# Packed attention, mixture of experts and soft mixture of experts in one fp32 kernel: the fold matrix made early, 4 KB weight rows and 32-row output matmuls in the tail

## The chip, the cores and the metric

One core of one Trainium2 chip runs the whole program. The metric is the device time of one execution in microseconds (us), the median of several runs. The kernel before the change was timed at 516.65 us (three runs, 515.19 to 517.91). TensorE (PE) multiplies, with PEld as its weight loads; VectorE (DVE), ScalarE (ACT) and GpSimd (POOL) do the rest, and SyncE (SP) issues nearly all DMAs.

## What is computed

```python
def sm_attn(qq, kk, vv):                      # softmax(q k^T / 8) v
    s = scale * np.matmul(qq, kk.transpose(0, 1, 3, 2))
    a = np.exp(s - np.max(s, axis=-1, keepdims=True))
    a = a / (np.sum(a, axis=-1, keepdims=True) + 1e-09)
    return np.matmul(a, vv)
p_packed = sm_attn(p, k, v)                   # 4 batches, 8 heads, 576 tokens, 32 packed, 64 wide
x = sm_attn(q, p_packed, p_packed)            # -> (2304, 512)

p = domain_probs / (domain_probs.sum(-1, keepdims=True) + 1e-09)
for e in range(4):                            # moe_w1 (4, 512, 1024), moe_w2 (4, 1024, 512)
    out += p[:, e:e+1] * (np.maximum(x @ w1[e], 0) @ w2[e])
x = out

logits = x @ phi                              # 32 slots = 8 experts x 4
d = softmax(logits, over the 2304 tokens);  slot_input = d.T @ x
slot_out[e] = np.maximum(slot_input[e] @ m1[e], 0) @ m2[e]     # m1 (8, 512, 1024), m2 (8, 1024, 512)
c = softmax(logits, over the 32 slots);     result = c @ slot_out          # (2304, 512)
```

All inputs and the output are fp32. In the program `w1`, `w2` are the weights of the first expert layer, `m1`, `m2` those of the second.

## The kernel before

The hidden values of the first expert layer are made in 128 slots: 4 batches (`b`), 8 chunks of 512 hidden columns each, 4 slots of 128 columns to a chunk. PE computes a slot in `mm1` (L620), ACT, DVE and POOL apply the ReLU and the gate (`ht`, L625 to L631), DVE turns the result (`flip_h`, L641) into `hr`, a ring of five places (`place(b, i)`), and PE adds to the logits (`logits`, L653). `softmaxes` (L677 and on) and `pooling` (L775) of a batch run inside the next batch's slots; `pooling` adds `d^T h` into `tacc`. `w2` isn't applied to tokens: it is multiplied with phi at the start (for the logits) and with the pooled `tacc` at the end.

For the last batch softmax and pooling have no later slots to hide in. That is the tail, in program order:

- `pooling(3)` on PE, then four DVE operations (L789) that rescale `tacc` and add;
- the rest of the last softmax: DVE (L743), POOL (L745), ACT (L749), DVE (L751 to L753), POOL (L755), DVE (L758) into `cts`;
- POOL makes `fold` (L1114), two stacked identities that add the two halves of the 128 partitions, then `sel` and zeros;
- **tt**: 16 matmuls of `tacc` with `fold` (L1133), in two halves of 8, copied out by DVE and by ACT (L1139);
- **si**: `tt` times `w2` (L1146), 32 matmuls; then `st2` (L1160 to L1175);
- **hid**: `st2` times `m1` (L1201), ReLU, eight transposes (`hidt`, L1219), `hm`;
- **so**: `hm` times `m2` (L1246): for experts 0 to 3 at the full width of 512 columns, for experts 4 to 7 in two parts of 256 columns. After each part come `so_sb`, `sr` (a matmul with `sel` that repeats the slots in four groups of 32 rows), `rr`, and the outputs: 18 matmuls with `ct` (L1284), copies to SBUF (`drain`, ACT and DVE in turn) and six DMAs of 384 KB.

The outputs use fp32r, a shortened format: in the trace an fp32r matmul leaves one record, an fp32 matmul two (the 16 of tt are 32 records). To keep fp32's precision, `ct` and `rr` are split in a high and a low part: the four 32-row groups hold hi, hi, lo, lo of `ct` against hi, lo, hi, lo of `rr`, so one 128-row matmul adds four products.

The tail's weights (`w2`, `m1`, `m2`) come as one stream of 80 chunks of 512 KB, on SP's queue in a fixed order: chunks 0 to 15 are `w2`, 16 to 47 `m1`, 48 to 63 the first half of `m2`, 64 to 71 and 72 to 79 the two parts of its second half. They use places of SBUF that come free (39 slots in all, `add_slots`). `fill_stream` starts them during the last batch; once all slots are taken, `load_chunk` issues chunk 39 and on, four at a time, when four chunks have been multiplied. So the first reload waits for the first eight matmuls of si, and SP, which works in order, holds everything behind it. A chunk of `w2` is read as two rows of 2 KB per partition, of `m1` as one of 4 KB, of `m2` as two of 2 KB (first half) or four of 1 KB:

```python
w2[e, 128 * x : 128 * x + 256, :].rearrange("(x p) d -> p x d", p=128)
```

`leftover(p, n, k)` is the end of ring place `p`, which no chunk uses.

Of the kernel before, what the change touches and what calls it, by code (L numbers as in the profile page):

```python
# [18 lines left out]
def tile_packed_attention_moe_softmoe(  # L19
# [102 lines left out]
    def place(b, i):  # L122
        return (NE * b + i) % RING
# [681 lines left out]
    for x in range(0, NFT, 2):  # L805
        for e in range(NE):
            chunks.append(
                w2[e, 128 * x : 128 * x + 256, :].rearrange("(x p) d -> p x d", p=128)
            )
# [72 lines left out]
    with tc.manual_schedule():  # L882
# [157 lines left out]
        for s in range(nslot):  # L1040
# [21 lines left out]
            if last == 0:  # L1062
                att.close()
                open_stream("s1", "right")
                for _ in range(2):
                    add_slots(1, a2_place)
            elif last == 8:
                hr_slots([place(NB, 0)])
            elif last == SPB - 3:
                add_slots(2, w1_place)  # L1070
# [27 lines left out]
        for _ in sg[b]:  # L1098
# [5 lines left out]
        tt = fin.tile([128, 2, NFT, 64], F32, tag="tt", name="tt")  # L1104
        ct = fin.tile([128, NB // 2, XR, 2, 2, 32], F32R, name="ct")
        rr_t = fin.tile([128, DM], F32R, name="rr")
        st2 = [
# [4 lines left out]
        sel = fin.tile([128, 128], F32, name="sel")  # L1112
        fold = fin.tile([128, 2, 32], F32, name="fold")
        pool.tensor_tensor(  # L1114
            out=fold,
            in0=ident.rearrange("p (a b s) -> p a b s", a=2, b=2)[:, :, 0],
            in1=ident.rearrange("p (a b s) -> p a b s", a=2, b=2)[:, :, 1],
            op=ALU.add,
        )
        si = leftover(0, DM)  # L1120
# [60 lines left out]

        chi = fin.tile([128, DF], F32R, tag="tt", name="chi")[:, :S]
        act.copy(chi, cts)
        for b in range(NB):
            src, hi = (
                t[32 * b : 32 * b + 32].rearrange("p (r x t) -> p x r t", r=2, t=32)
                for t in (cts, chi.bitcast(F32))
            )
# [26 lines left out]
        for i in range(2):  # L1215
            ps = mm_ps(f"hidt{i}")
            for j in range(4):
                o = 512 * i + 128 * j
# [21 lines left out]
        for s, d0, dw in so_steps:  # L1240
# [24 lines left out]
            act.copy(rr, sr[:, :dw])  # L1265
            for r0 in (32, 96):
                dve.tensor_tensor(  # L1267
                    out=rr[r0 : r0 + 32], in0=sr[r0 : r0 + 32, :dw],
                    in1=rr[r0 : r0 + 32].bitcast(F32), op=ALU.subtract,
                )  # L1270
            nb, nt = 512 // dw, 3
            for b2 in range(NB // 2):
# [4 lines left out]
                for j0 in range(0, XR, nt):  # L1277
                    jn = min(XR - j0, nt)
                    ob = out_tile()
                    for j in range(j0, j0 + jn, nb):  # L1280
                        m = min(nb, j0 + jn - j)
                        ps = mm_ps(f"o{d0}_{b2}_{j}")
                        for jl in range(m):
                            pe.matmul(  # L1284
                                ps[:, dw * jl : dw * jl + dw], cv[:, j + jl], rr,
                                start=True, stop=True,
                            )
                        drain(ob[:, dw * (j - j0) : dw * (j - j0 + m)], ps[:, : dw * m])
                    sp.dma_start(
# [33 lines left out]
```

## Time and profile before

| | us |
|---|---|
| median of three runs | 516.65 |
| the profiled execution, its own time | 512.97 |
| its span, first to last instruction | 511.2 |
| PE busy | 467.6 (91%) |
| DVE / POOL / ACT busy | 295.0 / 204.4 / 185.4 |
| mean granted TensorE clock | 0.962 of full speed |

The profiled execution is 3.68 us under the median of the runs. Nearly all idle time of PE lies in the tail, from about 419 us on; before it PE works without a gap (the stretch from 290 to 415 us shows 124.97 of 125 us busy). The tail has to be read on two lines at once: what PE waits for, and whether the 16 DMA engines move data. Times in rows are from the span's start.

### The profile page before, as it was taken

How to read it: one execution, taken by the hardware profiler on the slowest of the kernel's cores; microseconds unless marked ns; L12 is line 12 of the kernel's file. 1: busy time of each engine (PE TensorE's matmuls, PEld its weight loads, DVE VectorE, ACT ScalarE, POOL GpSimd, SP SyncE). 2: the span in 40 equal slices, each digit the busy share in tenths (PEclk: the TensorE clock that was granted, in tenths of full speed). 3: DMA queues.
4: the chain of work that ended last, by engine and by line, in shares of the span. 5: the costliest groups of instructions: out<-in, count | busy, mean ns of one | idle time of the engine just before them, and what ended most of it. 6: DMA issues, size and time to landing. Idle time of an engine off the chain costs nothing.

```text
span 511.2 us, 13177 instructions
## 1 busy us (share of the span) xinstructions
PE 467.6 (91%) x5572; PEld 332.1 (65%) x5572; DVE 295.0 (58%) x551; ACT 185.4 (36%) x446; POOL 204.4 (40%) x266
## 2 busy tenths in 40 slices
PE   6899899999999989999998999999999985999683
PEld 3778767778775767787665877865878755322142
DVE  4674346688762977778278788754866533140022
ACT  2476445434432433455133445432443200320023
POOL 3024333458743635595244449642765505000000
PEclk8799999999999999999998999999999996899986
DMA  8999634555430555732234522591934499699997
GB/s 200 388 315 288 255 131 140 139 133 166 139 112 3 164 159 147 184 132 86 82 130 130 131 83 83 179 345 58 357 136 165 163 346 418 267 403 394 385 382 251
DMA packets 61836, 104.36 MB, mean 204 GB/s; under 512 B 5904, under 2 KB 24848, under 8 KB 61776
## 3 DMA queue, kind: packets, MB, share of 16 engines
q1 hardware_dynamic: 61648, 103.36, 59.9%
q8 instruction: 44, 0.72, 0.6%
q0 software_dynamic: 128, 0.15, 0.2%
q14 instruction: 16, 0.13, 0.1%
HBM read 98.78 MB, written 4.72 MB: 202 GB/s over the span
## 4 chain that ended last, share of the span: by engine, by line
PE 69%; DMA 17%; DVE 6%; SPq 3%; ACT 2%; issue 1%; POOL 1%; ACTq 0%; POOLq 0%; DVEq 0%
PE h L620 36%; DMA w<-in_moe_w_dram 8%; PE pb L775 8%; PE lg L653 6%; PE g L585 6%; DMA hr<-in_moe_w_dram 4%; DMA ck<-in_moe_w_dram 3%; SPq L849 2%; PE w2t L260 2%; PE sa L358 2%; PE so L1246 1%; DMA hr<-in_v_dram 1%; PE tt L1133 1%; PE o L1284 1%; PE pw L275 1%; PE pv L455 1%
## 5 line engine op out<-in xcount | busy, mean ns | idle before, releaser
L631 POOL TENSOR_TENSOR ht<-ht,pe 128x288 f32<-128x288 f32 x192 | 153.0, 806 | 180.3 <-ACT ht L630 180.2
L620 PEld LDWEIGHTS h<-a,g 128*128 128x128 f32 x1536 | 206.6, 188 | 23.0 <-issue 14.6
L620 PE MATMUL h<-a,g 128*128 128x288 f32 x1536 | 221.6, 299 | 0.0
L630 ACT ACTIVATE ht<-h 128x288 f32<-128x288 f32 x192 | 79.0, 412 | 173.8 <-PE h L620 166.2
L641 DVE STREAM_TRANSPOSE hr<-ht 128x576 f32<-128x576 f32 x128 | 97.3, 763 | 45.2 <-POOL ht L631 41.8
L597 DVE TENSOR_TENSOR g<-g,g 128x512 fp32r<-128x512 f32 x64 | 40.9, 679 | 26.0 <-ACT g L595 26.0
L625 DVE SCALAR_TENSOR_TENSOR ht<-h,pe 128x288 f32<-128x288 f32 x64 | 28.0, 438 | 37.8 <-PE h L620 37.8
L595 ACT CAST g<-g 128x512 fp32r<-128x512 f32 x64 | 34.5, 589 | 28.5 <-PE g L585 28.5
L775 PE MATMUL pb<-hr,d 32*32 32x512 f32 x1152 | 40.6, 598 | 0.0
L585 PE MATMUL g<-w,pkn 64*32 64x512 f32 x512 | 35.8, 600 | 4.2 <-DMA w<-in_moe_w_dram 4.1
L653 PE MATMUL lg<-ht,wphi 128*32 128x288 f32 x512 | 38.3, 412 | 0.0
L653 PEld LDWEIGHTS lg<-ht,wphi 128*32 128x32 f32 x512 | 13.5, 109 | 33.2 <-POOL ht L631 22.5
L775 PEld LDWEIGHTS pb<-hr,d 32*32 32x32 f32 x1152 | 18.9, 103 | 14.3 <-issue 9.2
L1246 PE MATMUL so<-hr,hm 128*32 128x256 f32 (+1 forms) x136 | 18.5, 458 | 4.6 <-DMA hr<-in_moe_w_dram 4.6
L1267 DVE TENSOR_TENSOR rr<-sr,rr 32x256 fp32r<-32x256 f32 x4 | 1.7, 424 | 34.5 <-ACT rr L1265 34.5
L267 ACT COPY hr<-w2t 128x512 f32<-128x512 f32 x32 | 17.5, 598 | 5.3 <-PE w2t L260 5.2
L260 PE MATMUL w2t<-ident,hr 128*128 128x128 f32 x128 | 18.1, 288 | 0.2 <-ACT hr L267 0.2
L260 PEld LDWEIGHTS w2t<-ident,hr 128*128 128x128 f32 x128 | 15.4, 149 | 2.9 <-issue 0.9
L673 POOL COPY ps<-dpn 128x576 f32<-128x576 f32 x16 | 10.7, 667 | 13.5 <-DVE dpn L195 13.5
L789 DVE SCALAR_TENSOR_TENSOR tacc<-tacc,rsc,pb 128x512 f32<-128x512 f32 x12 | 8.2, 744 | 13.2 <-PE pb L775 13.2
L1246 PEld LDWEIGHTS so<-hr,hm 128*32 128x32 f32 x136 | 6.1, 116 | 13.5 <-DMA hr<-in_moe_w_dram 9.3
L1133 PE MATMUL tt<-fold,tacc 128*128 128x64 f32 x32 | 7.1, 423 | 7.7 <-POOL fold L1114 7.7
(161 smaller groups left out, 444.8 us busy)
## 6 DMA issues: line engine op xcount, KB each, us to landing
w<-in_moe_w_dram SPq DMA_DIRECT2D x32, 1024.0 KB, 5.1
hr<-in_moe_w_dram SPq DMA_DIRECT2D x40, 512.0 KB, 8.8
ck<-in_moe_w_dram SPq DMA_DIRECT2D x38, 512.0 KB, 7.6
hr<-in_moe_w_dram SPq DMA_DIRECT2D x8, 1024.0 KB, 9.9
k<-in_k_dram SPq DMA_DIRECT2D x16, 288.0 KB, 4.4
v<-in_v_dram SPq DMA_DIRECT2D x18, 192.0 KB, 6.3
q<-in_q_dram SPq DMA_DIRECT2D x12, 288.0 KB, 2.9
out_dram<-ob SPq DMA_DIRECT2D x8, 384.0 KB, 5.6
```

The lines of the kernel that those rows point to most:

```text
L260: pe.transpose(st[x][:, 128 * dc : 128 * dc + 128], t[:, x, 128 * dc : 128 * dc + 128], ident,)
L585: pe.matmul(ps[g][c : c + 32, :], pkn_t[b][o : o + 64, g, hp, 0, :], t[o : o + 64, 2 * g + hp, :], start=True, stop=True, tile_position=(o ...
L595: act.copy(gg[:, 0, g], ps[g])
L597: dve.tensor_tensor(out=gg[:, 1, g], in0=ps[g], in1=gg[:, 0, g].bitcast(F32), op=ALU.subtract)
L620: pe.matmul(ps[:, :HS], gg[:, l, g, fs], m[:, ts], start=(g == 0 and i == 0), stop=(g == 1 and i == 2),)
L625: dve.scalar_tensor_tensor(out=ht[:, ts], in0=ps[:, :HS], scalar=0.0, in1=pr[:, ts], op0=ALU.max, op1=ALU.mult,)
L630: act.activation(out=ht[:, ts], in_=ps[:, :HS], func=AF.Relu)
L631: pool.tensor_tensor(out=ht[:, ts], in0=ht[:, ts], in1=pr[:, ts], op=ALU.mult)
L641: dve.transpose(out=hr[:, place(b, i), :, f0 : f0 + 32], in_=ht_t[s].rearrange("p (x t) -> p x t", t=32),)
L653: pe.matmul(lg_t[b][r][32 * x : 32 * x + 32, :HS], wphi[:, NFT * e + 4 * hf + x, :], ht_t[4 * ci + x][:, HS * r : HS * r + HS], start=(ch ...
L775: pe.matmul(pb[c][m : m + 32, :], d[o, x + par, :], hr[o, lo : hi + 1 : hi - lo, x + par, :], start=(x == 0), stop=(x == NBLK - 2), tile_p ...
L1246: pe.matmul(so[32 * e : 32 * e + 32, d0 : d0 + dw], hm[s][:, x + xl, e, :], cks[e][:, dw * xl : dw * xl + dw], start=(s == 0 and x + xl == 0),
```

## The change

Four edits:

1. `fold` is made by POOL in slot 8 of the last batch, in the leftover of ring place 1, and no longer in the `fin` pool after the softmax.
2. `w2` chunks and those of the first half of `m2` are read as one row of 4 KB per partition (neighbouring rows of the matrix). So that the rows of `tt` and `hm` match, tt's stationary operand takes every second column of two blocks of `tacc`, and hidt's takes every fourth column of `hid`. The parts of `m2`'s second half keep 1 KB rows, of four neighbouring matrix rows.
3. The outputs are plain fp32: a matmul has 32 rows, three of them (tokens j, j+1, j+2 of a group) stand in row groups 0, 32 and 64 of the array and write three PSUM banks. The hi/lo split, `chi` and the two DVE subtractions on `rr` go; `ct` holds for each row group only its own third.
4. Each output matmul has its own copy of 256 columns, ACT and DVE in turn: nine each instead of six of 512 (ACT) and six of 256 (DVE) for one part.

```diff
-                w2[e, 128 * x : 128 * x + 256, :].rearrange("(x p) d -> p x d", p=128)
+                w2[e, 128 * x : 128 * x + 256, :].rearrange("(p x) d -> p x d", x=2)
...
-                    m2[4 * s + e, 128 * x : 128 * (x + nx), d0 : d0 + dw].rearrange(
-                        "(x p) d -> p x d", p=128
-                    )
+                    m2[4 * s + e, 512 * (x // 4) : 512 * (x // 4) + 512, d0 : d0 + dw].rearrange(
+                        "(p x) d -> p x d", x=4
+                    )[:, x % 4 : x % 4 + nx]
...
                 hr_slots([place(NB, 0)])
+                fold = leftover(place(NB, 0), 64)
+                pool.tensor_tensor(
+                    out=fold.rearrange("p (a s) -> p a s", a=2),
...
+                    op=ALU.add,
+                )
...
-        fold = fin.tile([128, 2, 32], F32, name="fold")
-        pool.tensor_tensor(
-            out=fold,
...
-                    tacc[:, NFT * e2 + x].rearrange("p a b -> p (a b)"),
-                    fold.rearrange("p a s -> p (a s)"),
+                    tacc[:, NFT * e2 + x // 2 * 2 : NFT * e2 + x // 2 * 2 + 2].rearrange(
+                        "p a b c -> p (a b c)"
+                    )[:, x % 2 : 256 : 2],
+                    fold,
...
-        chi = fin.tile([128, DF], F32R, tag="tt", name="chi")[:, :S]
-        act.copy(chi, cts)
+        nt = 3
         for b in range(NB):
...
-            for c in range(4):
+            src = cts[32 * b : 32 * b + 32].rearrange("p (r x t) -> p x r t", r=2, t=32)
+            for c in range(nt):
                 dst = ct[32 * c : 32 * c + 32, b // 2, :, b % 2]
-                if c < 2:
-                    act.copy(dst, src)
-                else:
-                    dve.tensor_tensor(out=dst, in0=src, in1=hi, op=ALU.subtract)
+                (act.copy if b % 2 else dve.tensor_copy)(dst[:, c::nt], src[:, c::nt])
...
-                pe.transpose(ps[:, 128 * j : 128 * j + 128], hid[:, o : o + 128], ident)
+                pe.transpose(
+                    ps[:, 128 * j : 128 * j + 128], hid[:, 512 * i + j : 512 * i + 512 : 4], ident
+                )
...
             act.copy(rr, sr[:, :dw])
-            for r0 in (32, 96):
-                dve.tensor_tensor(
-                    out=rr[r0 : r0 + 32], in0=sr[r0 : r0 + 32, :dw],
-                    in1=rr[r0 : r0 + 32].bitcast(F32), op=ALU.subtract,
-                )
...
-                    for j in range(j0, j0 + jn, nb):
-                        m = min(nb, j0 + jn - j)
-                        ps = mm_ps(f"o{d0}_{b2}_{j}")
-                        for jl in range(m):
-                            pe.matmul(
-                                ps[:, dw * jl : dw * jl + dw], cv[:, j + jl], rr,
-                                start=True, stop=True,
-                            )
-                        drain(ob[:, dw * (j - j0) : dw * (j - j0 + m)], ps[:, : dw * m])
+                    ps = [mm_ps(f"o{d0}_{b2}_{j0}_{j}", keep=True) for j in range(jn)]
+                    for j in range(jn):
+                        o = slice(32 * j, 32 * j + 32)
+                        pe.matmul(
+                            ps[j][:, :dw], cv[o, j0 + j], rr[o], start=True, stop=True,
+                            tile_position=(32 * j, 0),
+                        )
+                    for j in range(jn):
+                        drain(ob[:, dw * j : dw * j + dw], ps[j][:, :dw])
+                    let_go(ps)
```

How the change moves instructions is shown at two places. The first is POOL. At the tail of the kernel before, `fold` stands between the last softmax product (L755, `lt`) and `sel`:

```order
L631 TENSOR_TENSOR ht_5450<-ht_5450,pe_5173 128x288
L745 TENSOR_TENSOR lt_5527<-lt_5527,cm_5701 128x576
L755 TENSOR_TENSOR lt_5527<-lt_5527,cm_5701 128x576
L1114 TENSOR_TENSOR fold<-ident 128x64
L1124 COPY sel<-ident 128x16 x8
L1170 MEMSET hr 128x256 x4
L1172 MEMSET hm_5718 128x1024
```

In the changed kernel `sel` follows the softmax product at once:

```order
L631 TENSOR_TENSOR ht_5451<-ht_5451,pe_5174 128x288
L745 TENSOR_TENSOR lt_5528<-lt_5528,cm_5702 128x576
L755 TENSOR_TENSOR lt_5528<-lt_5528,cm_5702 128x576
L1124 COPY sel<-ident 128x16 x8
L1172 MEMSET hr 128x256 x4
L1174 MEMSET hm_5719 128x1024
```

and `fold` (written into `hr`) stands in slot 8 of the last batch, between the gate products (L631) of two slots:

```order
L631 TENSOR_TENSOR ht_4697<-ht_4697,pe_4323 128x288 x2
L631 TENSOR_TENSOR ht_4767<-ht_4767,pe_4323 128x288
L631 TENSOR_TENSOR ht_4840<-ht_4840,pe_4569 128x288 x2
L1070 TENSOR_TENSOR hr<-ident 128x64
L631 TENSOR_TENSOR ht_4892<-ht_4892,pe_4569 128x288
L745 TENSOR_TENSOR lt_4545<-lt_4545,cm_4886 128x576
```

So `fold` has moved ahead of the last 29 rows of POOL's list that belong to the slots and to the last softmax. The sixteen matmuls of tt stand at the same place on PE as before.

The second place is PE in the last part's outputs. Before, the 18 matmuls are in pairs that share a bank, and singles (o, first number the pair of batches, second the first token group):

```order
L1284 MATMUL o_0_5_6143<-rr,ct 128x256
L1284 MATMUL o_0_6_6147<-rr,ct 128x256 x2
L1284 MATMUL o_0_8_6151<-rr,ct 128x256
L1284 MATMUL o_1_0_6155<-rr,ct 128x256 x2
L1284 MATMUL o_1_2_6159<-rr,ct 128x256
L1284 MATMUL o_1_3_6163<-rr,ct 128x256 x2
L1284 MATMUL o_1_5_6167<-rr,ct 128x256
L1284 MATMUL o_1_6_6171<-rr,ct 128x256 x2
L1284 MATMUL o_1_8_6175<-rr,ct 128x256
```

Now each has its own bank (o, last number the row group):

```order
L1273 MATMUL o_0_3_0_6142<-rr,ct 128x256
L1273 MATMUL o_0_3_1_6143<-rr,ct 128x256
L1273 MATMUL o_0_3_2_6144<-rr,ct 128x256
L1273 MATMUL o_0_6_0_6152<-rr,ct 128x256
L1273 MATMUL o_0_6_1_6153<-rr,ct 128x256
L1273 MATMUL o_0_6_2_6154<-rr,ct 128x256
L1273 MATMUL o_1_0_0_6162<-rr,ct 128x256
L1273 MATMUL o_1_0_1_6163<-rr,ct 128x256
L1273 MATMUL o_1_0_2_6164<-rr,ct 128x256
```

The number of matmuls and of output DMAs has not changed; the copies behind them have (nine on ACT and nine on DVE for a part).

## Rows read from the trace of the kernel before

**Rows 1.** The chain of waits from 410 us: start us, us, what

```profile
410.14 8.75 PE pb L775 x250
419.00 2.72 DVE tacc L789 x4
...
426.11 1.15 POOL lt L755
```

**Rows 2.** Stretches of the tail: from:to us, busy us (x) by engine, PEclk, DMA share, GB/s

```profile
420.00:424.00 4.00, 0.00 (x0) 0.00 (x0) 2.68 (x6) 0.02 (x1) 1.16 (x1) 1.00 1.02 409
428.00:434.00 6.00, 6.00 (x30) 6.00 (x30) 1.08 (x4) 0.00 (x0) 3.41 (x11) 0.50 1.03 419
434.00:441.00 7.00, 7.00 (x49) 2.77 (x52) 0.00 (x0) 0.59 (x1) 0.00 (x0) 0.72 0.39 142
435.00:436.00 1.00, 1.00 (x5) 0.29 (x7) 0.00 (x0) 0.30 (x1) 0.00 (x0) 0.50 0.34 139
439.00:440.00 1.00, 1.00 (x13) 0.33 (x8) 0.00 (x0) 0.00 (x0) 0.00 (x0) 1.00 0.55 127
441.00:450.00 9.00, 7.77 (x75) 3.00 (x71) 4.90 (x14) 5.94 (x9) 0.00 (x0) 1.00 1.03 414
451.00:471.00 20.00, 18.98 (x141) 5.28 (x134) 2.65 (x6) 0.93 (x3) 0.00 (x0) 1.00 1.05 397
471.00:492.00 21.00, 14.27 (x89) 4.80 (x87) 1.00 (x3) 1.01 (x3) 0.00 (x0) 0.92 1.08 386
500.50:503.00 2.50, 2.03 (x13) 1.81 (x14) 1.53 (x4) 1.52 (x4) 0.00 (x0) 0.96 0.11 39
503.00:510.00 7.00, 1.34 (x7) 1.04 (x5) 1.27 (x3) 1.70 (x4) 0.00 (x0) 0.50 0.99 338
```

**Rows 3.** The timeline from 427 us: start us, us, instructions, [idle before <-releaser]

```profile
427.22 0.32 POOL L1114 TENSOR_TENSOR fold<-ident 128x64 f32<-128x64 f32 x1
427.30 0.77 DVE L758 STREAM_TRANSPOSE cts<-lt 32x576 f32<-32x576 f32 x1 [1.33 <-POOL lt L755]
427.59 7.09 PE L1133 MATMUL tt<-fold,tacc 128*128 128x64 f32 x32 [7.75 <-POOL fold L1114]
431.31 0.69 DVE L1139 COPY tt<-tt 128x512 f32<-128x512 f32 x1 [3.24 <-PE tt L1133]
434.61 6.06 PE L1146 MATMUL si<-ck,tt 128*32 128x512 f32 x34
434.72 0.59 ACT L1139 COPY tt<-tt 128x512 f32<-128x512 f32 x1 [10.05 <-PE tt L1133]
...
438.18 5.37 SPq L849 DMA_DIRECT2D ck<-in_moe_w_dram  x10
```

**Rows 4.** The timeline of POOL around slot 8 of the last batch

```profile
359.00 0.81 POOL L631 TENSOR_TENSOR ht<-ht,pe 128x288 f32<-128x288 f32 x1 [2.31 <-ACT ht L630]
```

**Rows 5.** Groups of instructions by form, 407 to 411 us | busy us, mean ns | idle

```profile
L1089 PE MATMUL idle<-ident 128*128 128x128 f32 x20 | 2.3, 273 | 0.0
```

**Rows 6.** Line L358 from 304 to 306 us: durations ns min/median/max, first and last start

```profile
L358 PE MATMUL sb<-qt,pkn x32: 401/401/425, 304.2 to 305.0; 32*32 32x288 f32 x32
```

**Rows 7.** The timeline of the last part and its outputs

```profile
496.45 0.11 PEld L1246 LDWEIGHTS so<-ck,hm 128*32 128x32 f32 x1 [0.42 <-DMA ck<-in_moe_w_dram]
498.83 0.70 PE L1263 MATMUL sr<-hr,sel 128*128 128x256 f32 x2 [0.46 <-ACT hr L1261]
499.56 0.37 ACT L1265 CAST rr<-sr 128x256 fp32r<-128x256 f32 x1 [0.79 <-PE sr L1263]
499.97 0.86 DVE L1267 TENSOR_TENSOR rr<-sr,rr 32x256 fp32r<-32x256 f32 x2 [5.28 <-ACT rr L1265]
500.97 3.37 PE L1284 MATMUL o<-rr,ct 128*128 128x256 f32 x18 [1.45 <-DVE rr L1267]
501.48 1.07 ACT L1237 COPY ob<-o 128x512 f32<-128x512 f32 x2 [1.55 <-PE o L1284]
501.60 0.78 DVE L1237 COPY ob<-o 128x256 f32<-128x256 f32 x2 [0.77 <-PE o L1284]
```

More of the change, by code (lines that the diff above doesn't have):

```diff
@@ L1068, in tile_packed_attention_moe_softmoe @@
                 hr_slots([place(NB, 0)])
+                fold = leftover(place(NB, 0), 64)
+                pool.tensor_tensor(
+                    out=fold.rearrange("p (a s) -> p a s", a=2),
+                    in0=ident.rearrange("p (a b s) -> p a b s", a=2, b=2)[:, :, 0],
+                    in1=ident.rearrange("p (a b s) -> p a b s", a=2, b=2)[:, :, 1],
+                    op=ALU.add,
+                )
             elif last == SPB - 3:
@@ L1104, in tile_packed_attention_moe_softmoe @@
         tt = fin.tile([128, 2, NFT, 64], F32, tag="tt", name="tt")
-        ct = fin.tile([128, NB // 2, XR, 2, 2, 32], F32R, name="ct")
-        rr_t = fin.tile([128, DM], F32R, name="rr")
+        ct = fin.tile([128, NB // 2, XR, 2, 2, 32], F32, name="ct")
+        rr_t = fin.tile([128, DM], F32, name="rr")
         st2 = [
@@ L1112, in tile_packed_attention_moe_softmoe @@
         sel = fin.tile([128, 128], F32, name="sel")
-        fold = fin.tile([128, 2, 32], F32, name="fold")
-        pool.tensor_tensor(
-            out=fold,
-            in0=ident.rearrange("p (a b s) -> p a b s", a=2, b=2)[:, :, 0],
-            in1=ident.rearrange("p (a b s) -> p a b s", a=2, b=2)[:, :, 1],
-            op=ALU.add,
-        )
         si = leftover(0, DM)
@@ L1180, in tile_packed_attention_moe_softmoe @@
                 )
-        chi = fin.tile([128, DF], F32R, tag="tt", name="chi")[:, :S]
-        act.copy(chi, cts)
+        nt = 3
         for b in range(NB):
-            src, hi = (
-                t[32 * b : 32 * b + 32].rearrange("p (r x t) -> p x r t", r=2, t=32)
-                for t in (cts, chi.bitcast(F32))
-            )
-            for c in range(4):
+            src = cts[32 * b : 32 * b + 32].rearrange("p (r x t) -> p x r t", r=2, t=32)
+            for c in range(nt):
                 dst = ct[32 * c : 32 * c + 32, b // 2, :, b % 2]
-                if c < 2:
-                    act.copy(dst, src)
-                else:
-                    dve.tensor_tensor(out=dst, in0=src, in1=hi, op=ALU.subtract)
+                (act.copy if b % 2 else dve.tensor_copy)(dst[:, c::nt], src[:, c::nt])
         hp = [mm_ps(f"hid{i}") for i in range(2)]
@@ L1217, in tile_packed_attention_moe_softmoe @@
             for j in range(4):
-                o = 512 * i + 128 * j
-                pe.transpose(ps[:, 128 * j : 128 * j + 128], hid[:, o : o + 128], ident)
+                pe.transpose(
+                    ps[:, 128 * j : 128 * j + 128], hid[:, 512 * i + j : 512 * i + 512 : 4], ident
+                )
             for s in range(2):
@@ L1265, in tile_packed_attention_moe_softmoe @@
             act.copy(rr, sr[:, :dw])
-            for r0 in (32, 96):
-                dve.tensor_tensor(
-                    out=rr[r0 : r0 + 32], in0=sr[r0 : r0 + 32, :dw],
-                    in1=rr[r0 : r0 + 32].bitcast(F32), op=ALU.subtract,
-                )
-            nb, nt = 512 // dw, 3
             for b2 in range(NB // 2):
@@ L1279, in tile_packed_attention_moe_softmoe @@
                     ob = out_tile()
-                    for j in range(j0, j0 + jn, nb):
-                        m = min(nb, j0 + jn - j)
-                        ps = mm_ps(f"o{d0}_{b2}_{j}")
-                        for jl in range(m):
-                            pe.matmul(
-                                ps[:, dw * jl : dw * jl + dw], cv[:, j + jl], rr,
-                                start=True, stop=True,
-                            )
-                        drain(ob[:, dw * (j - j0) : dw * (j - j0 + m)], ps[:, : dw * m])
+                    ps = [mm_ps(f"o{d0}_{b2}_{j0}_{j}", keep=True) for j in range(jn)]
[8 more added lines that the diff above has]
+                    let_go(ps)
                     sp.dma_start(
```

## The prediction

> **What bounds the kernel now.** In the last batch, up to 419 us, PE works without a gap (beside the table above), and of the four edits only `fold` and the `w2` loads fall there; so the tail is read. First the chain of waits [rows 1]: the last pooling matmul lets DVE add into `tacc` (four operations, done at 419.00 + 2.72 = 421.7), and from there the chain runs through the small steps of the last softmax to POOL's product at 426.11. Then the timeline [rows 3]: behind that product, in POOL's queue, stands `fold`, done at 427.54, and PE's tt starts at 427.59 after 7.75 us of idle time. The reader is to see that tt's other input, `tacc`, had been there for 5.9 us: tt waits for POOL's queue, not for data that the softmax makes.
>
> Next the stretches [rows 2]. The DMA engines move 419 GB/s while tt runs (428 to 434 us), run dry between 435 and 436 us (139 GB/s), flow again from 439 on (127 GB/s in that microsecond), and over 434 to 441 us move 142 GB/s. They stop because all 39 slots are full: SP issues the first reload at 438.18 [rows 3], 3.57 us after si's start at 434.61. From 441 on they run at 414, 397 and 386 GB/s, and PE waits for them: it is busy 14.27 of 21 us from 471 to 492. So from 441 us to the last weights the DMA stream is the bound, and the hole before it is lost time: at 414 GB/s the 7 us would move what takes 142 x 7 / 414 = 2.4 us, so **4.6 us** are lost.
>
> At the end the last weights land at about 496.45, then come `so_sb`, `sr`, `rr` and outputs [rows 7]; the outputs' DMAs run at 338 GB/s from 503 to 510 after a pause (39 GB/s from 500.5 to 503) [rows 2]. There the first copied group starts the last transfer, and the DMA ends the program.
>
> **Edit 1, fold.** In slot 8 it costs 0.32 us of POOL (its own row [rows 3]); POOL idles 2.31 us before its next product at 359.00 [rows 4], so it is free there; without that idle time it would be 0.32 us. Its wait, for the pooling of ring place 1, is over by then: the product ahead of it in POOL's queue needs a matmul that PE runs after that pooling. The 29 rows of POOL that it is moved past keep their order, and `sel` and the zeros come 0.3 us sooner, for which nothing waits.
>
> tt can then start when DVE's fourth addition ends, at about 421.8. The clock is still at its full level (2.4 GHz): granted 1.00 from 420 to 424, though PE has idled since 419, and 0.50 (1.2 GHz) only while tt ran [rows 2]. At half clock tt's 32 records took 7.09 us [rows 3], 0.22 each; twenty matmuls with weight loads of the same 128x128 size took 2.3 us at full clock [rows 5], 0.11 each. So tt takes 32 x 0.11 = 3.5 us and ends at 425.3. What is late next: DVE has to copy tt's first half, and in its queue the copy stands behind the transpose of `cts`, which waits for POOL's softmax product: 427.30 + 0.77 + 0.69 = 428.8 [rows 3]. The ACT copy is done before that. si starts at 428.8 and not at 434.6, **5.8 us** earlier.
>
> The edit also makes tt's weights strided (every second column). No row of this trace has a strided weight load. I bound its pace by the rows above: 0.11 (as now, full clock) and 0.44 (twice the half-clock pace). I take 0.11, the contiguous loads' value, because the loads' size is the same. The Trainium skill, "SBUF — State Buffer", section "Door 1: The DMA port swizzle", says that 16-byte lines are read at full rate when two reads hit each line: fp32 at stride 2 would be free, and hidt's stride 4 would not; no run here shows either, and the sum would stay. Hidt's eight transposes lie in a part of PE's work that is ahead of the stream, so I price them at nothing; without that cover, at twice the time, 8 x 0.11 = 0.9 us.
>
> If PE falls to half clock in its idle time up to 428.8, the first reload is issued 3.57 us later as now, at 432.4. From that issue (438.18) to data in the microsecond from 439 on pass under 1.8 us, so the new data are there by 434.2, before the queue runs dry after 435. So the hole closes whole: the gain is the smaller of 5.8 and 4.6, **4.6 us**. The rest only puts PE 1.2 us further ahead of the stream; si, hid and the slots that they free move with it, so the stream isn't starved later.
>
> **Edit 2, rows of 4 KB.** SP issues as many DMAs as before. `w2`'s chunks come while PE works without a gap: nothing. The 16 chunks of `m2`'s first half (8.39 MB) come in the DMA-bound stretch. `m1`, in rows of 4 KB, came at 419 and 414 GB/s, these in 2 KB at 397, the last ones in 1 KB at 386 [rows 2]. 8.39 MB at 397 take 21.1 us, at 414 20.3: **0.9 us** (0.86). The ends: nothing, and 1.1 us (at 419). I take the middle row, the nearest in time. The Trainium skill says in "DMA: Bandwidth & Descriptors", "Specifications", that transfers are at line rate from 512 B on; by that the sum would be 0.9 us less. The trace doesn't agree so far, 386 against 414 to 419, but other things differ between those stretches too, hence a rival.
>
> **Edits 3 and 4, outputs.** The two subtractions leave the path: PE's outputs wait 500.97 - 499.93 = 1.04 us from the end of `rr`'s copy on ACT [rows 7], of which a semaphore's 0.04 stays: -1.0 us. Against it, the first group of 384 KB is now ready 501.98 - 500.97 = 1.0 us after PE's start (copies of 512 and 256 columns on two engines [rows 7]). After the change it takes one fp32 matmul, three side by side, at most `sr`'s 0.70 us, and two ACT copies of 256 columns of 0.37 each, 1.4 us, while DVE makes one between: +0.4 to +0.6, I take +0.6. So **0.4 us**. Later groups come every 1.5 copies of DVE, 1.5 x 0.39 = 0.6 us, faster than the DMA takes them (393 KB at 338 GB/s, 1.16 us): nothing. The best end is 1.0. The worst: weight loads one after another at half clock, six records of 0.22 for a group (1.3 us), which makes the first group ready 1.4 us later than now and the five others 0.15 later each: 1.0 - 1.4 - 0.75 = -1.2. In the first part the same gain isn't on the path, as PE waits there for the last weights (496.45). The removal of `chi` and the cheaper `ct` copies lie on DVE and ACT beside hid: nothing.
>
> **Sum.** 4.6 + 0.9 + 0.4 = 5.9 us. Against the profiled execution that is 512.97 - 5.9 = 507.1 (span 505.3). That execution is 3.7 us under the median of the runs, so I carry the gain over: 516.65 - 5.9 = **510.7 us**, or 1.1% less. A measurement of this kernel can tell about 0.5%, 2.6 us, from no change.
>
> **Rivals.**
> - *Row length doesn't count* (a transfer at the same rate either way). For: 397 and 386 differ by only 3% although the row halves. Against: 419 and 414 for both stretches of 4 KB. Time: 516.65 - 5.0 = 511.6. Chance 0.13. By the Trainium skill's 512 B rule ("DMA: Bandwidth & Descriptors", "Specifications") it would come out so.
> - *Strided weights make tt slow, the hole stays.* It decides from a pace of about 0.27 on: tt then ends at 430.4, its ACT copy at 431.0, and at half clock the reload is issued at 434.6 and lands after the queue has run dry. At 0.44 tt ends at 435.9 and si starts at 436.5, 1.9 us later than now: 516.65 + 1.9 - 1.3 = 517.3, no change that can be measured. For: no row shows such a load. Against: it needs stride and clock both at their worst. Chance 0.08.
> - *The three row groups don't run side by side* (slower). Then 18 matmuls of `sr`'s kind take 18 x 0.70 = 12.6 us a part instead of 3.4 [rows 7]. The first part delays PE's last weights by some 8 us, the second the end by about 5 (of its 9, some 4 lie under the DMA as now): 516.65 + 13 - 5.5 = 524. It decides from about 0.36 us a matmul on (3 us a part, two parts, eat the gain). Against: 32 records of 288 columns in 32x32 tiles, 0.40 us each, start within 0.8 us [rows 6], four row groups among them. Chance 0.05.
> - *PE stays at half clock through the outputs*, and the outputs' worst end holds: 516.65 - 5.5 + 1.2 = 512.4; if the matmuls on the last weights run so too, the 1.9 us from 496.45 to 498.4 [rows 7] double, 514.3. For: the clock is 0.50 again from 503 on [rows 2]. Against: 0.96 just before. Chance 0.08.
>
> **How the numbers follow.** The forecast keeps 0.66. Its own range, terms at their ends and the runs' spread of 1.4 us around the median, goes down to 516.65 - 4.6 - 1.1 - 1.0 - 1.4 = 508.5. Upward, row length at nothing and the outputs at their worst give 516.65 - 4.6 + 1.2 = 513.3, and with 0.7 of spread 514.0; this takes in the first and most of the fourth rival, and leaves out the second and third. Faster by over 0.5% (under 514.1): forecast, first rival and nearly all of the fourth, 0.86. Within 0.5%: the second and the rest, 0.09. Slower: the third, 0.05.
>
> **What would show it.** Right: tt starts within 0.2 us of DVE's last addition and not after POOL; si near 428.8, behind DVE's copy; no stretch under 350 GB/s between 428 and 441 us; the stretch of `m2`'s first half at 410 GB/s or more; no subtraction between `rr` and the outputs, whose first DMA goes out some 0.4 us sooner after the last weights. Wrong: tt lasting over 8 us, a hole in the DMA left, the same 397 GB/s, an output part that holds PE longer than 6 us, or any new wait of PE before 419 us.

## The result and the profile after

| | before | after |
|---|---|---|
| median, us | 515.92 (4 runs, 514.84 to 517.91) | 507.42 (4 runs, 506.40 to 507.49) |
| profiled execution, own time, us | 512.97 | 507.49 |
| its span, us | 511.2 | 505.7 |

The ratio is 0.987, with a 95% interval of 0.983 to 0.990: faster by 5.1 to 8.7 us, clear of no change though less than 2%. (The two medians alone give 0.984.) Some executions show a lower clock and take over 1.5% longer than the fastest of their kernel; the ratios here and below leave these out, the medians and run counts don't. The forecast was 5.9 us less and 510.7 us; the median lies 3.3 us under that and 1.1 us under the low end of the range (508.5), which was set from 516.65. Profile against profile, the sum said 507.1 us and the profiled execution took 507.49.

The chain of waits of the changed kernel, from 411 us on (start us, us, what):

```profile
411.02 8.80 PE pb L775 x250
...
419.92 2.79 DVE tacc L789 x4
422.71 0.14 DVE den L735
422.85 6.98 PE tt L1133 x32
429.84 4.95 PE si L1148 x26
434.79 7.85 DMA ck<-in_moe_w_dram
...
490.00 3.63 PE so L1242 x64
```

Where POOL's product and `fold` stood before [rows 1, rows 3], tt now follows DVE's fourth addition at 422.71 by 0.14 us. The end of that addition is called T0 from here on: 421.72 in the execution profiled before, 422.71 in this one. The code ahead of it is the same but for `fold` and `w2`'s loads, so times counted from T0 can be set side by side.

The timeline (start us, us, instructions, [idle before <-releaser]):

```profile
422.85 6.98 PE L1133 MATMUL tt<-hr,tacc 128*128 128x64 f32 x32 [2.09 <-DVE den L735]
...
428.28 0.77 DVE L758 STREAM_TRANSPOSE cts<-lt 32x576 f32<-32x576 f32 x1 [1.33 <-POOL lt L755]
429.08 0.69 DVE L1141 COPY tt<-tt 128x512 f32<-128x512 f32 x1
...
429.83 1.06 PE L1148 MATMUL si<-ck,tt 128*32 128x512 f32 x1
...
433.42 7.06 SPq L849 DMA_DIRECT2D ck<-in_moe_w_dram  x10
```

si starts at T0 + 7.12 us, before it was T0 + 12.89 [rows 3]; SP's first reload goes out at T0 + 10.71, before at T0 + 16.46. DVE's copy of tt stands behind its transpose of `cts`, as foreseen, and releases si.

The stretches (from:to us, busy us (x) of PE, PEld, DVE, ACT and POOL, the granted clock, DMA share, GB/s):

```profile
428.00:434.00 6.00, 6.00 (x32) 3.34 (x35) 1.78 (x4) 2.68 (x7) 4.12 (x15) 0.57 1.02 418
434.00:441.00 7.00, 5.96 (x55) 2.87 (x47) 0.79 (x2) 0.00 (x0) 0.00 (x0) 1.00 1.02 411
...
446.00:467.00 21.00, 19.78 (x146) 5.67 (x138) 1.05 (x3) 0.93 (x3) 0.00 (x0) 1.00 1.03 414
468.00:489.00 21.00, 15.32 (x110) 6.35 (x109) 2.31 (x7) 2.87 (x9) 0.00 (x0) 0.92 1.09 384
495.00:498.00 3.00, 2.73 (x25) 1.92 (x25) 1.68 (x5) 1.86 (x6) 0.00 (x0) 1.00 0.49 170
```

The 7 us that moved 142 GB/s [rows 2] now move 411. `m2`'s first half comes at 414 in place of 397, and the 1 KB rows of its second half at 384, before 386. What is left of idle DMA time is the pause ahead of the last outputs, 170 GB/s over 3 us.

The end (timeline):

```profile
494.08 0.70 PE L1259 MATMUL sr<-hr,sel 128*128 128x256 f32 x2 [0.49 <-ACT hr L1257]
494.82 0.37 ACT L1261 COPY rr<-sr 128x256 f32<-128x256 f32 x1 [0.79 <-PE sr L1259]
495.24 4.45 PE L1273 MATMUL o<-rr,ct 32*128 32x256 f32 x31 [0.46 <-ACT rr L1261]
495.97 0.92 ACT L1233 COPY ob<-o 128x256 f32<-128x256 f32 x3 [0.78 <-PE o L1273]
496.02 0.81 DVE L1233 COPY ob<-o 128x256 f32<-128x256 f32 x2 [5.56 <-PE o L1273]
496.65 1.35 SPq L1280 DMA_DIRECT2D out_dram<-ob  x2
```

No subtraction stands between `rr` and the outputs. The first output DMA goes out 2.57 us after `sr`'s start, where it took 3.27 before (`sr` at 498.83 [rows 7]):

```profile
502.10 1.56 SPq L1289 DMA_DIRECT2D out_dram<-ob  x2
```

### The profile page after: what moved, and what is told of

Read it like the earlier page. It is cut to its first block, busy times and chain, and to the rows that moved or that the text cites. A ratio compares the mean times of both kernels' runs of the same rounds, so it can differ in the third digit from the quotient of the medians.

```text
span 505.7 us, 13249 instructions
## 1 busy us (share of the span) xinstructions
PE 472.3 (93%) x5608; PEld 334.9 (66%) x5608; DVE 290.9 (58%) x551; ACT 181.7 (36%) x449; POOL 204.4 (40%) x266
## 4 chain that ended last, share of the span: by engine, by line
PE 77%; DMA 12%; DVE 6%; SPq 3%; ACT 1%; issue 1%; ACTq 0%; DVEq 0%
PE h L620 39%; PE pb L775 8%; PE lg L653 7%; PE g L585 6%; DMA ck<-in_moe_w_dram 4%; DMA hr<-in_moe_w_dram 4%; DMA w<-in_moe_w_dram 4%; PE pv L455 3%; PE sa L358 2%; PE o L1273 2%; SPq L849 2%; PE w2t L260 2%; PE sb L358 2%; PE et L419 1%; PE tt L1133 1%; PE so L1242 1%
## 5 line engine op out<-in xcount | busy, mean ns | idle before, releaser
L631 POOL TENSOR_TENSOR ht<-ht,pe 128x288 f32<-128x288 f32 x192 | 153.1, 807 | 180.0 <-ACT ht L630 179.8
L1233 DVE COPY ob<-o 128x256 f32<-128x256 f32 x12 | 4.7, 422 | 36.5 <-PE o L1273 36.2
L1242 PE MATMUL so<-ck,hm 128*32 128x512 f32 (+1 forms) x52 | 12.3, 531 | 1.1 <-DMA ck<-in_moe_w_dram 1.1
```

The costliest lines, as they stand in the source:

```text
L631: pool.tensor_tensor(out=ht[:, ts], in0=ht[:, ts], in1=pr[:, ts], op=ALU.mult)
L1242: pe.matmul(so[32 * e : 32 * e + 32, d0 : d0 + dw], hm[s][:, x + xl, e, :], cks[e][:, dw * xl : dw * xl + dw], start=(s == 0 and x + xl == 0),
```

## The experiments

The tail, T0 to the end of the span, is 89.5 us in the profile before and 83.0 after, 6.5 us shorter; the head, up to T0, is 1.0 us longer. The forecast of the three terms was 5.9, while the medians moved by 8.5. So the first question was where 2 to 3 us more come from. Theory A: one of the edits gives them, outside the terms of the sum. Theory B: no edit does; the runs of the kernel before scatter, and three or four of them gave a median that was too high.

**First set: the whole change, and three of its parts alone.** e0_whole is the changed kernel. The others are the kernel before with one part; e1_fold:

```diff
+                fold = leftover(place(NB, 0), 64)
+                pool.tensor_tensor(
...
-        fold = fin.tile([128, 2, 32], F32, name="fold")
-        pool.tensor_tensor(
```

e2_rows:

```diff
-                 w2[e, 128 * x : 128 * x + 256, :].rearrange("(x p) d -> p x d", p=128)
+                 w2[e, 128 * x : 128 * x + 256, :].rearrange("(p x) d -> p x d", x=2)
...
+                        "(p x) d -> p x d", x=4
...
+                     )[:, x % 2 : 256 : 2],
...
+                    ps[:, 128 * j : 128 * j + 128], hid[:, 512 * i + j : 512 * i + 512 : 4], ident
```

e3_outputs:

```diff
-        chi = fin.tile([128, DF], F32R, tag="tt", name="chi")[:, :S]
...
-                    out=rr[r0 : r0 + 32], in0=sr[r0 : r0 + 32, :dw],
...
+                            ps[j][:, :dw], cv[o, j0 + j], rr[o], start=True, stop=True,
+                            tile_position=(32 * j, 0),
```

What was expected of e0_whole, e1_fold, e2_rows and e3_outputs, in this order:

> The whole change again, beside its parts on one chip. The two profiled executions differ by 5.5 us (512.97 to 507.49), the medians by 8.5 (515.92 to 507.42); some 3 us of the gain are in no row read so far. Theory A (the extra belongs to an edit): about -8.5 us here, and one of the three single edits shows 3 us more than its term. Rival theory B (the profiled execution of before was a good one among runs that scatter, and nothing of an edit): the kernel before scatters by 2 to 3 us on this chip too, this one by under 1.2, and the gain against the fastest run of before is about 6.

> Edit 1 alone. By the sum: -4.6 us, the DMA's hole between 434 and 441 us gone, si some 5.8 us earlier. If the 3 us of theory A belong to the hole (a clock or a DMA restart that is worse in most runs than in the profile): about -7.5. Rival, the hole only moves to a later stretch: under -2.

> Edit 2 alone (w2 and half of m2 in rows of 4 KB, with the strided weights of tt and hidt). By the sum: -0.9 us, and 410 to 415 GB/s instead of 397 while the first half of m2 comes; the hole stays as it is. If the 3 us belong to w2's loads beside the slots of the last batch: about -4. Rival, row length doesn't count: 0, 397 GB/s.

> Edits 3 and 4 alone (outputs as fp32 matmuls of 32 rows, each with its own copy). By the sum: -0.4 us, first output DMA of a part 1.5 to 1.7 us after PE's start instead of 1.0 to 1.3, no subtraction. If the 3 us belong here: about -3.5. Rival, the longer hold of PE in the first part's outputs costs as much as the subtractions: 0.

Measured, beside 23 runs of the kernel before with a median of 514.51 us:

| kernel | median, us | ratio, 95% | T0, us | tail, us | `sr` of the last part, from T0 | `sr` to the end |
|---|---|---|---|---|---|---|
| before (profile shown ahead) | | | 421.7 | 89.5 | 77.1 | 12.4 |
| e0_whole | 508.61 | 0.9875 (0.985 to 0.990) | 422.8 | 83.8 | 72.2 | 11.6 |
| e1_fold | 510.46 | 0.9928 (0.990 to 0.995) | 421.8 | 84.3 | 71.8 | 12.5 |
| e2_rows | 514.35 | 0.9995 (0.997 to 1.002) | 423.3 | 89.5 | 77.3 | 12.2 |
| e3_outputs | 513.51 | 0.9974 (0.995 to 1.000) | 428.1 | 88.7 | 77.1 | 11.6 |

The profile of e3_outputs is of an execution of 518.47 us, 5 us above the median; only its tail is compared.

No part alone gives 2 to 3 us outside the tail: theory A finds no edit. T0 differs by 6 us between these executions without regard to the edits, and the kernel before has its median 2 us under the three runs first shown. Theory B stands in this, but two of its details missed: the changed kernel scatters too (507.63 to 515.47 us), and its median is only 3.6 us under the fastest run of before (512.22), where 6 was expected. `fold` shortens the tail by 5.2 us, the outputs by 0.8. The rows alone gave nothing in the tail, though `m2`'s first half came faster (403 GB/s, where 410 to 415 was expected); the stretches of e2_rows show why:

```profile
437.00:441.00 4.00, 4.00 (x25) 1.41 (x27) 0.00 (x0) 0.00 (x0) 0.00 (x0) 0.62 0.09 23
441.00:446.00 5.00, 4.51 (x43) 1.44 (x35) 0.40 (x1) 0.35 (x1) 0.00 (x0) 1.00 0.90 318
452.00:472.00 20.00, 19.10 (x146) 5.61 (x139) 3.48 (x7) 0.92 (x3) 0.00 (x0) 1.00 1.03 403
```

The hole is there as before (23 GB/s), and when the stream came back it ran at 318 GB/s for 5 us; that costs about as much as the rows give, (414 - 318) x 5 / 414 = 1.2 us.

**Second set: two parts together, and two changes of the output phase.** Is a part worth the same whichever other part is there? e5_fold_rows is the whole change with the outputs as before, e6_fold_outs the whole change with the weight rows as before (diffs as above). Two more start from the whole change and ask what bounds the outputs now. In e7_banks they may use all eight PSUM banks:

```diff
-    idle_since = [-1] * 6
+    idle_since = [-1] * 8
+    nbank = [6]
...
+        nbank[0] = 8
```

In e8_late two output groups of the first part are held back into the last part:

```diff
+            if late:
+                out_group(*late.pop(0))
             sr = mm_ps(f"sr{d0}")
...
+            for args in late:
+                out_group(*args)
+            late = []
...
+                groups, late = groups[:-2], groups[-2:]
```

> Edits 1 and 2 of the change (fold in slot 8; w2 and half of m2 in 4 KB rows), outputs left as before. Theory A, the terms add up, each on the same chain of transfers: the tail (from the end of DVE's last addition to the span's end) is that of the fold edit alone, 84.3 us, less the 0.9 of the rows, 83.4; the median is 510.5 - 0.9 = 509.6 beside the same kernel before, ratio about 0.991. Theory B, the rows only shift a wait (the rows alone measured -0.3 us, its tail 89.5 like before's): tail 84.3, ratio 0.993, and the part of m2 read in 4 KB rows would still show over 405 GB/s. Against the whole change (ratio 0.9875) this run leaves out the outputs: by A those are then worth the 0.8 us that their own run showed in the tail, by B 2 to 2.5 us.

> Edits 1, 3 and 4 (fold in slot 8; outputs as fp32 matmuls of 32 rows), the weight rows as before. Theory A, terms add up: tail 84.3 - 0.8 = 83.5 us, m2's first half at 397 GB/s; median about 509.7, ratio 0.9912, and the rows are then worth 0.9 us between this run and the whole change. Theory B, the rows are worth more once the hole is closed, since the transfers then set the end all the way: the distance to the whole change is over 1.5 us.

> The whole change, and the output phase may use all eight banks instead of six, so that two groups of three side by side fit beside the sum that is kept. Theory P, the first part's groups are held by the copies out of the banks: the 18 matmuls take about 3.3 us in place of 4.55, the last part's sums end 1 us sooner and so does the kernel, ratio to the whole change 0.998. Theory Q, TensorE is busy with the matmuls themselves (it shows busy 1.00 from 487 to 493 us): 4.4 to 4.6 us as before, no difference.

> The whole change, and the first part's last two output groups are held back until the last part's sums are made: one is computed before sr, one before the last part's first group. Theory P, TensorE's hold in the first part's outputs now sets when the last part's outputs begin, and the DMAs idle for it (245, 114 and 153 GB/s from 495 to 498 us, about 1.9 us of transfers): the sums end 1.5 us sooner, the held groups fill the hole, the tail falls from 83.0 to 83.8 by 1 to 1.5 us, to about 82. Theory Q, the last part's sums then wait for their weights, since the transfers are the bound there: no difference, or up to 0.5 us later by the matmuls put in the way.

Measured, beside 19 runs of the kernel before with a median of 513.92 us:

| kernel | median, us | ratio, 95% | tail, us | `sr` of the last part, from T0 | `sr` to the end |
|---|---|---|---|---|---|
| e5_fold_rows | 509.05 | 0.9904 (0.987 to 0.994) | 84.3 | 71.8 | 12.5 |
| e6_fold_outs | 508.99 | 0.9913 (0.988 to 0.995) | 83.5 | 71.9 | 11.6 |
| e7_banks | 507.27 | 0.9875 (0.984 to 0.991) | 82.8 | 71.3 | 11.5 |
| e8_late | 508.95 | 0.9910 (0.988 to 0.994) | 86.0 | 73.6 | 12.4 |

The medians of e5 and e6 fit the additive theory (509.6 and 509.7 expected), but the interval of e5 holds the rival's 0.993 as well, and its tail of 84.3 us is the one that the rival forecast. The rows' price shows best in the stretch that holds `m2`'s first half. First e6_fold_outs, which differs from the whole change (414 GB/s, shown above) by its rows of 2 KB alone:

```profile
451.00:471.00 20.00, 19.16 (x159) 5.77 (x152) 0.97 (x3) 0.92 (x3) 0.00 (x0) 1.00 1.05 397
```

Then e1_fold, with rows of 2 KB too:

```profile
446.00:466.00 20.00, 19.37 (x162) 5.75 (x151) 2.80 (x6) 0.92 (x3) 0.00 (x0) 1.00 1.05 397
```

And e5_fold_rows, which differs from e1_fold by its rows of 4 KB alone, with the stretch of its profile in which the gain was lost again:

```profile
434.00:441.00 7.00, 5.73 (x56) 2.14 (x52) 1.06 (x5) 2.23 (x4) 0.00 (x0) 0.99 0.97 351
446.00:466.00 20.00, 19.55 (x158) 5.72 (x150) 2.59 (x6) 0.92 (x3) 0.00 (x0) 1.00 1.03 414
```

The rate is 397 and 414, the two numbers of the forecast. It is the length of the rows that counts and not that they are neighbours alone: the parts of `m2`'s second half became neighbouring rows too, of 1 KB as before, and their rate stayed at 384 to 386. Counted from T0, the ten megabytes behind the 8th take 25.0 us in the four profiled kernels with rows of 2 KB and 24.1 to 24.2 us in seven of the ten profiles with rows of 4 KB: 0.8 us less. The other three (e2_rows, and e4_no_fold and e7_banks with a microsecond or two at 287 to 369 GB/s in it) took 24.5 to 24.7. In e5 the slow stretch came earlier, 351 GB/s in place of 411 to 417, about 1.1 us, and its tail is no shorter than e1's. Such stretches stood in four profiles with the new rows (e2, e4, e5, e7) and in none of the four with the old ones; whether the rows cause them or chance does, these runs don't settle.

e7 speaks for theory P in its place: the first part's 18 output matmuls hold TensorE from 484.28 to 487.70, 3.42 us, where they held it 4.48 in the profile after (485.45 to 489.93). Its timeline:

```profile
484.28 3.50 PE L1275 MATMUL o<-rr,ct 32*128 32x256 f32 x36 [0.46 <-ACT rr L1263]
485.01 3.07 ACT L1235 COPY ob<-o 128x256 f32<-128x256 f32 x9 [0.79 <-PE o L1275]
485.05 3.19 DVE L1235 COPY ob<-o 128x256 f32<-128x256 f32 x9 [27.25 <-PE o L1275]
```

With six banks, one of them kept by `so`, only five are free for groups of three, and TensorE waits for copies although the views call it busy. The kernel need not gain by it, as the last sums then wait for their weights:

```profile
490.42 0.11 PEld L1244 LDWEIGHTS so<-ck,hm 128*32 128x32 f32 x1 [0.84 <-DMA ck<-in_moe_w_dram]
```

The next set asked for the medians.

e8 fits neither theory: its last sums began at T0 + 67.0 us, hardly sooner than the 67.2 of the profile after, and took 6.1 us in place of 3.7, with a granted clock of 0.50 for most of them. So the longer tail of this profile is put down to the clock, and whether holding groups back would help stays open.

**Third set: repeats on one chip, the change without `fold`, and tt at the higher clock.** e10_whole_again is the changed kernel, e11_banks_again is e7's. e4_no_fold is the whole change with the lines on `fold` put back as before. e9_warm adds idle matmuls to the whole change, ahead of tt:

```diff
+        wp = mm_ps("warm2")
+        for _ in range(28):
+            pe.transpose(wp[:, :128], ident, ident)
```

> The whole change again, beside the other three of this call on one chip. Theory B of the first call (the gain is the tail's, 6 us, and what went beyond it in the first comparison was scatter of the kernel before) expects a ratio of 0.987 to 0.989 and a tail of 82.9 to 83.9 us. Theory A (an edit gives 3 us more outside the tail) expects 0.983 and a first addition of the tail that ends under 420 us in the profiled run.

> The whole change with eight banks in the output phase, now on the same chip as the whole change. The run before showed a tail of 82.75 us and a median that its scatter can't set apart. Theory Q (TensorE's own matmuls are the hold) expects no difference to the whole change, within 0.2%; theory P (the copies out of the banks hold it) expects 0.5 to 1 us less.

> Edits 2, 3 and 4 without the first: fold is made after the last batch as before, so the transfers should again stop between 434 and 441 us. Theory A, the terms add up whatever the order: before less 0.9 for the rows and 0.8 for the outputs, tail 87.8 us, ratio 0.9967. Theory B, fold is the one that counts, rows and outputs are worth little by themselves: tail 88.6 (the outputs alone showed that), ratio 0.998 to 1.0. The distance to the whole change is what the fold edit is worth as the last of the edits: 4.8 us by A, 5.5 or more by B.

> The whole change, and 28 transposes that nothing reads are put on TensorE just ahead of tt, so that its clock need not be at the lower level when tt runs. Theory H, the half clock of tt costs nothing, since si waits for VectorE's copy of tt: the clock is 1.00 during more of tt and si, and the tail stays within 0.5 us of 83.0 to 83.8, unless the added transposes make tt start later (some 3 us of them at the lower clock, which would show as tt that much later and the tail longer by up to 3 us, less what tt gains). Theory K, the half clock of tt is on the path: tt lasts about 3.5 us in place of 7, si starts 2 us or more sooner and the tail is shorter by over 1 us.

Measured, beside 21 runs of the kernel before with a median of 514.47 us:

| kernel | median, us | ratio, 95% | T0, us | tail, us | `sr` of the last part, from T0 |
|---|---|---|---|---|---|
| e10_whole_again | 509.06 | 0.9890 (0.985 to 0.994) | 427.5 | 84.9 | 73.2 |
| e11_banks_again | 507.47 | 0.9883 (0.983 to 0.994) | 420.2 | 83.1 | 71.5 |
| e4_no_fold | 514.27 | 0.9996 (0.997 to 1.003) | 423.8 | 88.2 | 76.6 |
| e9_warm | 510.52 | 0.9907 (0.988 to 0.994) | 424.6 | 85.9 | 74.2 |

The whole change is at 0.989, as theory B of the first set had it. Without `fold` all but nothing of it is left, and the hole is back (437 to 443 us of e4_no_fold):

```profile
437.00:443.00 6.00, 6.00 (x41) 2.02 (x43) 0.00 (x0) 2.48 (x7) 0.00 (x0) 0.75 0.32 115
```

As the last of the edits `fold` is worth 514.27 - 509.06 = 5.2 us, the same that its tail showed alone; by the two intervals it can be 2.8 us more or less. e4's tail of 88.2 lies between the two theories' 87.8 and 88.6; from its last `sr` to the end pass 11.6 us, as in every profile with the new outputs in the order of the change.

The eight banks can't be told from six by the medians: 507.47 and 509.06 on the same chip, but with intervals that overlap for nearly all of their width, and 0.9875 for both e0 and e7 on two chips. The shorter hold was there again (3.4 us). The two tails, 82.8 and 83.1, lie at the low end of the three of the whole change, 83.0, 83.8 and 84.9. That eight banks beat six is not shown, and the landing of the last weights speaks against it where the clock is 1.00. In the traces of the eleven profiles with that clock, the last sums end 1.96 to 2.00 us after the last chunk has landed, whether the first part's outputs held TensorE 2.93, 3.42 or 4.48 us.

e9's timeline shows tt at the higher clock:

```profile
422.81 3.00 PE L1132 MATMUL warm<-ident 128*128 128x128 f32 x26
425.65 3.88 PE L1136 MATMUL tt<-hr,tacc 128*128 128x64 f32 x32
...
430.93 0.69 DVE L1144 COPY tt<-tt 128x512 f32<-128x512 f32 x1
...
431.68 1.94 PE L1151 MATMUL si<-ck,tt 128*32 128x512 f32 x8 [2.15 <-DVE tt L1144]
```

tt took 3.88 us in place of 6.98, TensorE then idled 2.15 us for DVE's copy, and si began at T0 + 7.13, where it begins in the whole change too (7.12). Theory H holds: tt's lower clock costs nothing. The other profiles say the same: in the ten with the early `fold` tt lasted 3.88 to 7.06 us, and si began at T0 + 7.12 to 7.14 in each. The longer tail comes from the last part, where the clock was low, as in e10. There it reads (stretches of e10_whole_again; before them `o` of the first part starts at 489.50):

```profile
489.00:492.00 3.00, 2.52 (x20) 2.01 (x20) 1.12 (x3) 1.41 (x5) 0.00 (x0) 0.82 1.09 385
492.00:499.00 7.00, 7.00 (x69) 4.32 (x68) 2.67 (x7) 2.12 (x6) 0.00 (x0) 0.59 1.09 382
499.00:503.00 4.00, 3.04 (x36) 1.46 (x28) 0.32 (x1) 1.11 (x4) 0.00 (x0) 1.00 0.62 215
```

and its chain of waits:

```profile
489.50 1.13 PE o L1273 x10
...
490.66 4.90 PE o L1273 x23
495.56 4.73 PE so L1242 x64
...
500.74 0.71 PE sr L1259 x2
```

The first part's outputs hold TensorE 6.0 us here instead of 4.5, the last sums 4.7 instead of 3.7, and no DMA is waited for. The last `sr` comes at T0 + 73.2 us, 1.8 later than in the profile after. Of that 0.6 us are the transfers, as the last chunk landed at T0 + 69.5 and not 68.9; 1.2 us are TensorE's, whose sums end 3.2 us after that chunk and not 2.0.

## Why the prediction was right, and where it was off

**fold, 4.6 us.** Right in each step. tt starts 0.14 us after DVE's last addition, si waits for DVE's copy behind the transpose and starts at T0 + 7.12 (forecast 428.8 - 421.7 = 7.1), 5.77 us earlier (5.8), and the hole closes whole. In transfers: the 8th megabyte from T0 on has come at 23.8 us before and at 19.2 to 19.3 in three profiles of the whole change, 4.6 us earlier. The three other profiles without the early `fold` have it at 23.9 to 24.9: there the first reload comes at T0 + 16.4 to 16.5 whatever has been loaded, so the hole is longer when the stream was further on by T0, and in e2 the slow stretch follows. Up to the landing of the last weights e1 had 0.3 MB less to move than the profile before (0.8 us at 400 GB/s); with that the 5.2 us of e1's tail and the 4.6 of the forecast go together. The one wrong detail is the clock: tt was to run at the higher level, and ran at 0.50 in 6.98 us. It changed nothing, as e9 shows by giving tt that level.

**The strided weights of tt.** 6.98 / 32 = 0.218 us a record at the lower clock, against 0.22 with contiguous ones [rows 3], and 3.88 / 32 = 0.121 at the higher, against the 0.11 taken over from contiguous loads [rows 5]. The second rival is out. The Trainium skill's "SBUF — State Buffer", "Door 1: The DMA port swizzle", had fp32 at stride 2 at full rate, and the trace agrees.

**Rows, 0.9 us.** Right in mechanism and nearly in size: 397 against 414 GB/s, 0.8 us where the transfers are the bound. The first rival, that row length doesn't count, is out. By the Trainium skill's "DMA: Bandwidth & Descriptors", "Specifications", transfers are at line rate from 512 B on; here 1 KB, 2 KB and 4 KB rows ran at 384 to 386, 397 and 414 GB/s, so the measurement decides against it. What the forecast did not see is that a single profile, or a median with an interval of 0.3%, need not show it. Slow stretches of 1 us came and went, and between T0 and the landing of the last weights the DMA engines had 27.5 to 28.2 MB to move in the fourteen profiles, worth 1.6 us at 400 GB/s, more than this term.

**Outputs, 0.4 us.** A term mis-sized on the safe side. `sr`'s start to the first output DMA fell from 3.27 to 2.57 us, 0.7, and `sr` to the end of the span from 12.2 to 12.5 us (four profiles with the old outputs) to 11.5 to 11.7 (nine with the new ones, e8 and its other order left out), 0.8. The step that failed is the +0.6 taken for the first group: it is ready for its DMA 496.65 - 495.24 = 1.41 us after TensorE's start, inside the 1.4 to 1.6 of the forecast, but the old one was ready after 1.13 and not 1.0 (its DMA went out at 502.10, the start was 500.97 [rows 7]); so +0.3. The third rival is out: three row groups do run side by side, 18 matmuls in 4.5 us and not 12.6.

That "in the first part the same gain isn't on the path, as PE waits there for the last weights" held at the clock of 1.00. In the profile after, TensorE goes from the first part's outputs, which hold it 4.48 us where 18 matmuls held it 2.93 before, straight into the last sums. But these end 2.00 us after the last weights have landed, and 1.96 in the ten other profiles at that clock: the longer hold cost 0.04 us at most there.

**The lower clock at the end**, the fourth rival, was priced at 1.9 us for the last sums. It came in the profiles of e8, e9 and e10, where the last sums ended 3.2 to 4.8 us after the last weights and not 2.0, so it cost 1.2 to 2.8 us. It is part of the spread of the changed kernel rather than a fixed cost.

**The sum.** Measured terms: 4.6 + 0.8 + 0.8 = 6.2 us, or 6.8 with the 5.2 of e1's tail for `fold`. The ratios of three comparisons, 0.987, 0.9875 and 0.989, make 5.7 to 6.9 us. The 5.9 of the forecast lies within. That the profiled execution met its 507.1 to 0.4 us is in part luck: the tail gained 6.5 us and the head lost 1.0.

**The step that failed** is the last: "That execution is 3.7 us under the median of the runs, so I carry the gain over: 516.65 - 5.9". The median of three runs was taken for the kernel's, and its 516.65 was high: 19 to 23 runs on three chips have medians of 513.9 to 514.5. From 514.3 the same gain gives 508.4; the changed kernel's medians were 507.4, 508.6 and 509.1. The range's low end hung on 516.65 as well. Whether chance or the chip of the first runs, which is not on record, made them high stays open. Most of the scatter is in the head: T0 lay between 420.2 and 428.1 us in fourteen profiles, and between 420.2 and 427.5 in the seven whose code ahead of it is the same (after, e0, e5, e7, e8, e10, e11). Its cause is open too. The clock near the start does not order it, as two of the seven show; first e11_banks_again, with T0 at 420.2,

```profile
10.00:20.00 10.00, 7.52 (x96) 5.92 (x89) 7.70 (x20) 4.46 (x15) 0.67 (x1) 0.70 1.08 337
```

then e10_whole_again, with T0 at 427.5 and the higher clock:

```profile
10.00:20.00 10.00, 6.74 (x90) 4.20 (x78) 7.40 (x20) 3.00 (x10) 0.00 (x0) 1.00 1.08 317
```

## What to carry to other kernels

When a transfer stream stops because its slots are full, look for the first instruction that frees one and follow its inputs back: here a constant that takes 0.3 us to make, queued on another engine behind the softmax, cost 4.6 us, and every later edit was worth under 1. Measure the parts against a point inside the program (here the last addition before the tail) when the head scatters by more than the edits are worth, and put the forecast on the gain, since the median of three runs can be 2 us off. When a stage gets faster, ask what is next: after the hole was closed the transfers still set the end, so a shorter hold of TensorE gave nothing that could be shown, and only its lower clock made the last sums later.

## What was not expected of the hardware

- The granted clock in the last part differs between executions of one program: 1.00 while the first part's outputs and the last sums ran in the profile after, 0.59 on average over 7 us of them in e10, the same kernel. There the last sums ended 3.2 us after the last weights and not 2.0.
- The row length of a transfer counts beyond 1 KB: 384 to 386, 397 and 414 GB/s for 1, 2 and 4 KB (2 and 4 KB in the same stretch, 1 KB in a later one).
- Weight loads with a stride of two fp32 values cost nothing, with a stride of four they do: the eight transposes of `hidt` show it at a clock of 1.00. Weight loads of the kernel before, then of the changed kernel, over the stretch from 438 to 462 us (busy us, mean ns | idle us, releasers):

```profile
L1219 PEld LDWEIGHTS hidt<-ident,hid 128*128 128x128 f32 x8 | 0.8, 140 | 1.3 <-ACT hid L1213 0.9 <-DVE hid L1214 0.4
```

```profile
L1213 PEld LDWEIGHTS hidt<-ident,hid 128*128 128x128 f32 x8 | 1.1, 209 | 1.2 <-ACT hid L1208 0.9 <-DVE hid L1209 0.3
```

  8 loads take 1.1 us in place of 0.8; the last weights come later all the same, so the sum needed no term for it.
- A TensorE that the views call busy without a gap can still be held by copies: eight banks in place of six took the same 36 records of `o` from 4.48 to 3.42 us.
